# Sliding-window attention and a leaky-ReLU MLP on one core: queries and keys transposed from two row groups of the PE array

## The chip, the cores and the metric

The kernel runs on one NeuronCore of a Trainium2 chip. The core has a matrix engine (PE, whose weight loads are listed apart as PEld), a vector engine (DVE), a scalar engine (ACT), a general engine (POOL) and a queue that issues DMAs (SP); POOL can issue DMAs as well. Each engine works through its own list of instructions in order and waits on semaphores for the others. The metric is device time in microseconds. Before the change it was 356.27 us, the median of 3 runs (355.5 to 356.88).

## The reference

Eight batches of eight heads, 576 tokens, head dimension 64. Each token attends to the tokens at most 32 away; the result goes through a two-layer MLP with a leaky ReLU.

```python
scores = scale * np.matmul(q, k.transpose(0, 1, 3, 2))        # [8, 8, 576, 576], scale = 1/8
mask = np.abs(pos[:, None] - pos[None, :]) <= 32
attn = softmax(np.where(mask, scores, -1e9))
x = np.matmul(attn, v)                                        # to [4608, 512]: heads side by side
h = x @ w_in                                                  # [4608, 2048]
out = np.maximum(0.01 * h, h) @ w_out                         # [4608, 512], float32
```

## The kernel before, in words

Heads are taken in pairs: pair `p` holds heads `p` and `p + 4`, so that the two heads' 64 dimensions fill 128 rows. There are four pairs (`NPAIR`) in each of eight batches (`B`).

**Loads.** `load_qk` (L63 to L74) fetches q and k of a pair into two tiles, `qf` and `kf`, of 96 partitions; partition `i` holds six (`RUN`) consecutive tokens of both heads, two runs of 1536 bytes. Each tile is one DMA of 288 KB on SP's queue. `load_v` (L76 to L86) uses two DMAs, each into 64 partitions. When `behind` is given, a DMA of one element from a weight tile is first put into the tile that will be loaded (L69), so that the load, which overwrites that element, can't start before those weights have landed. Batch 1's q and k are held back in this way behind a part of `w_in`.

**Casts.** `cast_qk` (L163) turns a pair's q and k into bf16 tiles `qb` and `kb`, on POOL; for batches 0 and 1 the q half runs on DVE. The heads' dimensions are brought side by side in the same instruction. `cast_v` (L169) writes v into block-diagonal tiles `vbd`.

**Transposes.** `transposes` (L177 to L208) is a generator that issues its work piece by piece. For each pair and for q, then k, it issues six PE transposes of 96 rows by 128 columns into one PSUM tile `tp`, and ACT copies the tile out: q into `qT` (L195), k into `kT` (L201), from which DVE fills the block-diagonal `kbd` (L204). Each `next` of the generator does q or k of one pair. For batches 0 and 1 `tp` comes from the ring `mmps` of three PSUM buffers that the MLP's matmuls use; for later batches it comes from `tps`, a pool of one buffer of its own.

**Attention.** A step `i` covers half a sequence of one pair. `score(i)` issues five matmuls, ACT's exponential (L226) and POOL's mask product (L230). `weighted(i)` issues two matmuls for the sums (L238, L239), five for the values (L246), DVE's reciprocal (L252) and DVE's product into `xT` (L254).

**MLP.** `h_tile` (L259 to L268) is four matmuls with 256 or 384 token columns and ACT's leaky ReLU; `o_tile` (L270 to L281) is sixteen matmuls of 512 columns, a DVE copy, and the store.

**Order.** Everything is issued in an order written out in the program; there is no scheduler. The first part, from L344 on, is straight-line code for batch 0 and batch 1. After it the MLP is cut into chunks, and before each chunk `step()` (L306) is called as often as a rate and the chunk's needed tokens ask. A step issues the next score, then its own weighted sum, and around them the transposes of the next batch up to the count in `PLAN`, then the casts and loads that `PLAN` lists for later batches. `state["tp"]` counts pieces of the generator, eight per batch.

Of the kernel before, what the change touches and what calls it, by code (L numbers as in the profile page):

```python
# [9 lines left out]
FP32 = mybir.dt.float32  # L10
BF16 = mybir.dt.bfloat16
AF = mybir.ActivationFunctionType
# [4 lines left out]
def kernel(  # L17
# [12 lines left out]
    nc = tc.nc  # L30

    B, H, S, D = q.shape
# [5 lines left out]
    NPAIR = H // 2  # L38
# [20 lines left out]

    qf, kf, vf = {}, {}, {}  # L60
    RUN = S // 96

    def load_qk(b, p, behind=None):  # L63


        for into, src, name in ((qf, q, "qf"), (kf, k, "kf")):
            t = fload.tile([96, 2, RUN * D], FP32, name=f"{name}{p}")
            if behind is not None:
                nc.sync.dma_start(out=t[0:1, 0, 0:1], in_=behind.bitcast(FP32))  # L69
                behind = None  # L70
            nc.sync.dma_start(  # L71
                out=t, in_=src[b, p:H:NPAIR].rearrange("a (p c) d -> p a (c d)", c=RUN),
            )
            into[b, p] = t  # L74

    def load_v(b, p, behind=None):  # L76

# [22 lines left out]
    ident = const.tile([128, 128], BF16)  # L100
# [5 lines left out]
    nc.vector.memset(ones_bd[64:128, 64:128], 1.0)  # L106


    qb = const.tile([96, NPAIR, RUN, 2, D], BF16)
    kb = const.tile([96, NPAIR, RUN, 2, D], BF16)  # L110
# [26 lines left out]
    for lo in (0, 64):  # L137
        w = win[lo:lo + 64]
        nc.gpsimd.affine_select(
            out=w, in_=w, compare_op=ALU.is_ge, fill=0.0,  # L140
# [3 lines left out]
            out=w, in_=w, compare_op=ALU.is_ge, fill=0.0,  # L144
# [15 lines left out]

    qT = {}

    def cast_qk(b, p, q_eng=None):  # L163
        for eng, src, dst in ((q_eng or nc.gpsimd, qf, qb), (nc.gpsimd, kf, kb)):
            eng.tensor_copy(  # L165
                out=dst[:, p], in_=src[b, p].rearrange("p a (c d) -> p c a d", d=D),
            )
# [9 lines left out]
    def transposes(b, first=False):  # L177

        qT[b] = attn.tile([128, NPAIR, S], BF16, name="qT")
        for p in range(NPAIR):  # L180
            for which, src in (("q", qb), ("k", kb)):
                if first:
                    tp = mmps.tile([128, RUN, 96], BF16, name="tp0", tag="mm")
                else:
                    tp = tps.tile([128, RUN, 96], BF16, name="tp")
                for c in range(RUN):
                    nc.tensor.transpose(  # L187
                        tp[:, c],
                        src[:, p, c].rearrange("p a d -> p (a d)"),
                        ident[0:96, 0:96],  # L190
                    )

                tok = tp.rearrange("p c i -> p i c")
                if which == "q":
                    nc.scalar.activation(  # L195
                        out=qT[b][:, p].rearrange("p (i c) -> p i c", c=RUN), in_=tok, func=AF.Copy,
                    )
                else:
                    kT = attn.tile([128, S], BF16, name="kT")
                    kT_v = kT.rearrange("p (i c) -> p i c", c=RUN)  # L200
                    nc.scalar.activation(out=kT_v, in_=tok, func=AF.Copy)  # L201
                    for a in range(2):
                        r = slice(64 * a, 64 * a + 64)
                        nc.vector.tensor_copy(  # L204
                            out=kbd[b % 2][r, p, :, r],
                            in_=kT[r].rearrange("p (n j) -> p n j", j=64),
                        )
                yield  # L208

    probs = {}  # L210

# [3 lines left out]
    def score(i):  # L215
        b, hf, p = where(i)
        ps = scps.tile([128, 1024], FP32, name="ps")
        c0 = 512 - HALF
        for blk, q0, n in WIN[hf]:
            nc.tensor.matmul(  # L220
                ps[:, c0:c0 + n], kbd[b % 2][:, p, blk],
                qT[b][:, p, q0:q0 + n], start=True, stop=True,
            )
# [58 lines left out]


    NC = 2 * NPAIR * B
    state = {"tp": 8, "done": 0}
    t_parts = {}

    PLAN = (
        ((0, 0, 0, 0, 0, 2, 4, 6), ((), (), (), (), (0,), (1, 2), (3,), ()),
         ((), (), (), (), (), (), (0,), (1, 2, 3))),
        ((0, 1, 2, 3, 4, 5, 6, 7), ((0,), (1,), (2,), (3,), (), (), (), ()),
         ((), (), (), (), (0,), (1,), (2,), (3,))),
    )

    def step_transposes(upto):
        while state["tp"] < min(upto, 8 * B):
            b = state["tp"] // 8  # L300
# [43 lines left out]
    first = transposes(0, first=True)  # L344

    def first_pair():
        next(first)
        next(first)

    cast_qk(0, 0, nc.vector)  # L350
    make_masks()
    cast_qk(0, 1, nc.vector)
    first_pair()
    first_pair()
    clear(vbd[0], 2)
    cast_v(0, 0)
    cast_qk(0, 2, nc.vector)
    score(0)
    load_w_in(0, 512)
    first_pair()  # L360
    clear(vbd[0], 3)
    cast_qk(0, 3, nc.vector)
    load_w_in(512, 1024)
    for i in range(NPAIR):
        score(i + 1)
        if i + 1 < NPAIR:
            cast_v(0, i + 1, on_act=True)
        if i < 2:
            load_w_in(1024 + 512 * i, 1536 + 512 * i)
        else:  # L370
            load_w_out(i - 2)
        weighted(i)
        if i == 0:
            first_pair()
    state["done"] = NPAIR


# [10 lines left out]
        if f % 4 == 3:  # L388
            nc.gpsimd.memset(kbd[1][:, f // 4], 0.0)
    for p in range(NPAIR):  # L390
        cast_qk(1, p, nc.vector)
    for p in range(NPAIR):
        load_v(1, p, w_out_bf[0:1, 4, 0:2] if p == 0 else None)
    second = transposes(1, first=True)
    for f in range(FFC):
        h_tile(256, 256, f)
        if f % 4 == 3:
            next(second)
            next(second)
            nc.gpsimd.memset(vbd[1][:, f // 4], 0.0)  # L400
    state["tp"] = 16
    score(8)
    for p in range(NPAIR):
        if p < 3:
# [69 lines left out]
```

The softmax here doesn't subtract the row's maximum and nothing guards it: scores larger than these inputs give would overflow.

## Time and profile before

| what | value |
|---|---|
| median of 3 runs | 356.27 us |
| the profiled execution, and its span | 355.59 us, 353.9 us |
| PE busy, share of the span | 324.3 us, 92% |
| weight loads (PEld) | 208.2 us, 59% |
| DVE, ACT, POOL busy | 211.8, 183.4, 178.7 us |
| DMA packets, MB | 60707, 42.37 MB |
| transposes, q and k (L187) | 2 x 192, 14.4 us busy each, mean 214 ns |
| evictions of q and k on ACT (L195, L201) | 2 x 32, mean 649 and 650 ns |
| POOL casts of k and q (L165) | 32 of 834 ns, 24 of 820 ns |
| median from issue to landing of q, k, v loads | 3.5, 3.9, 3.4 us |

Busy time of PE is a sum of records that overlap, because matmuls are pipelined: one transpose's record lasts 214 ns, while a row of six takes less than half of six times that. How long a row of matmuls really takes is read from the start of one to the start of what follows. The granted clock of PE was full throughout the execution (every digit of the page's clock row is 9).

### The profile page before, as it was taken

To read this page: it belongs to the slowest core of one execution; us is meant where nothing else is said; L and a number is where in the kernel's file an instruction comes from. 1 tells how busy PE (TensorE), PEld (TensorE's weight loads), DVE (VectorE), ACT (ScalarE), POOL (GpSimd) and SP (SyncE) were. 2 spreads that over 40 slices of the span, in tenths; PEclk is the share of its full clock that TensorE was granted. 3 is DMA by queue.
4 is the path that set the end of the run, shared out by engine and by line. 5 is a ranking of instruction groups with operands and counts; after the bars stand their busy time and mean duration, and the time that the engine had idled before them with its cause. 6 is when DMAs were issued, how large, how long until landed. Compare 5 with 4: busy or idle time off the path is not lost.

```text
span 353.9 us, 6635 instructions
## 1 busy us (share of the span) xinstructions
PE 324.3 (92%) x2600; PEld 208.2 (59%) x2624; DVE 211.8 (60%) x242; ACT 183.4 (52%) x363; POOL 178.7 (51%) x213
## 2 busy tenths in 40 slices
PE   2658998999989898999999898999999999999995
PEld 1437864584957655656656555656656656555472
DVE  5588647757686877645653778554676676630101
ACT  5765862292845637518527527716528517326060
POOL 7797676578765766524543568533655423200000
PEclk9999999999999999999999999999999999999999
DMA  8999986599995274342453265340010010020101
GB/s 187 214 205 236 269 162 182 144 201 235 209 255 146 58 222 133 69 126 88 140 162 70 63 177 165 88 124 33 0 61 30 2 61 31 5 86 0 61 31 59
DMA packets 60707, 42.37 MB, mean 120 GB/s; under 512 B 39684, under 2 KB 56068, under 8 KB 60676
## 3 DMA queue, kind: packets, MB, share of 16 engines
q1 hardware_dynamic: 56388, 37.76, 42.7%
q0 software_dynamic: 4288, 4.20, 7.2%
q8 instruction: 20, 0.33, 0.4%
q14 instruction: 11, 0.09, 0.1%
HBM read 36.70 MB, written 9.44 MB: 130 GB/s over the span
## 4 chain that ended last, share of the span: by engine, by line
PE 77%; DMA 7%; DVE 6%; POOL 4%; SPq 2%; issue 2%; ACT 1%; DVEq 0%; POOLq 0%; ACTq 0%
PE mm L273 33%; PE mm L264 31%; DMA kf<-in_k_dram 7%; DVE r L252 5%; PE x L246 3%; PE tp L187 3%; PE ps L220 3%; PE s L238 2%; PE s L239 2%; SPq L71 1%; POOL vbd L175 1%; POOL vbd L400 1%; SPq L82 1%; DVE xT L254 1%; POOL pr L230 1%
## 5 line engine op out<-in xcount | busy, mean ns | idle before, releaser
L252 DVE RECIPROCAL r<-s 128x288 f32<-128x288 f32 x64 | 125.1, 1954 | 38.5 <-PE s L239 38.2
L230 POOL TENSOR_TENSOR pr<-e,mask 128x544 bf16<-128x544 bf16 x64 | 77.7, 1213 | 115.0 <-ACT e L226 114.7
L264 PE MATMUL mm<-xT,w_in_bf 128*128 128x384 bf16 (+1 forms) x896 | 132.7, 304 | 0.9 <-ACT kT L201 0.8
L268 ACT ACTIVATE gT<-mm 128x384 bf16<-128x384 f32 (+1 forms) x224 | 99.0, 445 | 63.0 <-PE mm L264 58.6
L273 PE MATMUL mm<-w_out_bf,gT 128*128 128x512 bf16 x552 | 126.8, 379 | 1.3
L264 PEld LDWEIGHTS <-w_in_bf 128*128 128x128 bf16 x896 | 86.6, 98 | 38.0 <-issue 1.3
L273 PEld LDWEIGHTS <-gT 128*128 128x128 bf16 x576 | 54.9, 98 | 61.1
L226 ACT ACTIVATE e<-ps 128x544 bf16<-128x544 f32 x64 | 39.8, 622 | 77.6 <-PE ps L220 77.6
L280 DVE COPY o_sb<-mm 128x512 f32<-128x512 f32 x36 | 24.9, 691 | 66.8 <-PE mm L273 66.8
L204 DVE COPY kbd<-kT 64x576 bf16<-64x576 bf16 x64 | 28.4, 444 | 18.2 <-ACT kT L201 17.6
L175 POOL CAST vbd<-vf 64x576 bf16<-64x576 f32 x58 | 38.3, 661 | 1.9
L254 DVE TENSOR_TENSOR xT<-x,r 128x288 bf16<-128x288 f32 x64 | 29.3, 458 | 7.0 <-PE mm L264 0.5
L165 POOL CAST kb<-kf 96x768 bf16<-96x768 f32 x32 | 26.6, 834 | 9.5 <-DMA kf<-in_k_dram 9.5
L246 PE MATMUL x<-pr,vbd 128*128 128x128 bf16 (+2 forms) x320 | 26.9, 217 | 2.0 <-POOL vbd L175 1.0
L220 PE MATMUL ps<-qT,kbd 128*128 128x128 bf16 (+2 forms) x320 | 27.3, 219 | 0.3
L238 PE MATMUL s<-pr,ones_bd 128*128 128x288 bf16 x64 | 19.0, 297 | 8.7 <-DVE r L252 7.0
L220 PEld LDWEIGHTS <-kbd 128*128 128x128 bf16 x320 | 21.1, 102 | 8.1 <-issue 0.6
L195 ACT ACTIVATE qT<-tp 128x576 bf16<-128x576 bf16 x32 | 20.8, 649 | 9.6 <-PE tp L187 9.0
L246 PEld LDWEIGHTS <-vbd 128*128 128x128 bf16 x320 | 21.4, 101 | 7.1 <-issue 2.8
L201 ACT ACTIVATE kT<-tp 128x576 bf16<-128x576 bf16 x32 | 20.8, 650 | 8.9 <-PE tp L187 7.9
L187 PE MATMUL tp<-ident,qb 96*128 96x96 bf16 x192 | 14.4, 214 | 8.5 <-DVE qb L165 6.7
L165 POOL CAST qb<-qf 96x768 bf16<-96x768 f32 x24 | 19.7, 820 | 0.0
(31 smaller groups left out, 107.7 us busy)
## 6 DMA issues: line engine op xcount, KB each, us to landing
qf<-in_q_dram SPq DMA_DIRECT2D x32, 288.0 KB, 3.5
kf<-in_k_dram SPq DMA_DIRECT2D x32, 288.0 KB, 3.9
vf<-in_v_dram SPq DMA_DIRECT2D x64, 144.0 KB, 3.4
out_dram<-o_sb SPq DMA_DIRECT2D x36, 256.0 KB, 2.2
w_in_bf<-in_moe_w_in_dram POOLq DMA_DIRECT2D x8, 256.0 KB, 6.4
w_out_bf<-in_moe_w_out_dram POOLq DMA_DIRECT2D x4, 512.0 KB, 13.5
qf<-w_in_bf SPq DMA_DIRECT2D x1, 0.0 KB
vf<-w_out_bf SPq DMA_DIRECT2D x1, 0.0 KB
```

Source lines behind the costliest of these rows:

```text
L165: eng.tensor_copy(out=dst[:, p], in_=src[b, p].rearrange("p a (c d) -> p c a d", d=D),)
L175: nc.gpsimd.tensor_copy(out=vbd[b % 2][r, p, :, r], in_=vf[b, p][r])
L204: nc.vector.tensor_copy(out=kbd[b % 2][r, p, :, r], in_=kT[r].rearrange("p (n j) -> p n j", j=64),)
L220: nc.tensor.matmul(ps[:, c0:c0 + n], kbd[b % 2][:, p, blk], qT[b][:, p, q0:q0 + n], start=True, stop=True,)
L226: nc.scalar.activation(out=e, in_=ps[:, 512 - HALF:512 - HALF + NCOL], func=AF.Exp, scale=scale,)
L230: nc.gpsimd.tensor_mul(pr, e, mask[hf])
L246: nc.tensor.matmul(x[:, a:a + n], vbd[b % 2][:, p, blk, :], pr[:, c0:c0 + n], start=(n_ == 0), stop=(n_ == len(WIN[hf]) - 1), skip_group_c ...
L252: nc.vector.reciprocal(r, s)
L254: nc.vector.tensor_mul(xT[:, p, t0:t0 + HALF], x, r)
L264: nc.tensor.matmul(h[:, 0:n], w_in_bf[:, c, ts(f, 128)], xT[:, c, ds(t0, n)], start=(c == 0), stop=(c == DMC - 1),)
L268: nc.scalar.activation(out=gT[t0][:, f, 0:n], in_=h[:, 0:n], func=AF.Prelu, alpha=0.01)
L273: nc.tensor.matmul(o, gT[t0][:, f, ts(j, 128)], w_out_bf[:, f, :], start=(f == 0), stop=(f == FFC - 1),)
```

## The change

q and k of a pair now share one tile, `qkf`: q on partitions 0 to 63, k on 64 to 127. A partition holds nine consecutive tokens of both heads, two runs of 2304 bytes, and `RUN` is 9. The bf16 copies share `qkb` likewise. One cast on POOL covers both; for batches 0 and 1 it is split into 64 rows on DVE and 64 on POOL. With `behind`, both halves get the one-element DMA.

A transpose now takes 64 rows and gives 64 columns. q's transposes are placed in rows 0 to 63 of the PE array and k's in rows 64 to 127, and are issued in turn, nine of each, into two PSUM tiles. These come from the ring `mmps` in all batches; the ring has four buffers, and the pool `tps` is gone. Each `next` of the generator does a whole pair, so the counts in `PLAN` and `state["tp"]` are halved, and `step` issues transposes in one place, after the weighted sum.

```diff
-    mmps = ctx.enter_context(tc.tile_pool(name="mmps", bufs=3, space=PS))
+    mmps = ctx.enter_context(tc.tile_pool(name="mmps", bufs=4, space=PS))
...
-    tps = ctx.enter_context(tc.tile_pool(name="tps", bufs=1, space=PS))
-    RUN = S // 96
+    RUN = S // 64
...
-        for into, src, name in ((qf, q, "qf"), (kf, k, "kf")):
-            t = fload.tile([96, 2, RUN * D], FP32, name=f"{name}{p}")
+        t = fload.tile([128, 2, RUN * D], FP32, name=f"qkf{p}")
+        for w, src in enumerate((q, k)):
             if behind is not None:
-                nc.sync.dma_start(out=t[0:1, 0, 0:1], in_=behind.bitcast(FP32))
-                behind = None
+                nc.sync.dma_start(out=t[64 * w:64 * w + 1, 0, 0:1], in_=behind.bitcast(FP32))
             nc.sync.dma_start(
-                out=t, in_=src[b, p:H:NPAIR].rearrange("a (p c) d -> p a (c d)", c=RUN),
+                out=t[64 * w:64 * w + 64],
+                in_=src[b, p:H:NPAIR].rearrange("a (p c) d -> p a (c d)", c=RUN),
             )
...
-    def cast_qk(b, p, q_eng=None):
-        for eng, src, dst in ((q_eng or nc.gpsimd, qf, qb), (nc.gpsimd, kf, kb)):
-            eng.tensor_copy(
-                out=dst[:, p], in_=src[b, p].rearrange("p a (c d) -> p c a d", d=D),
+    def cast_qk(b, p, split=False, eng=None):
+        parts = ((nc.vector, 0, 64), (nc.gpsimd, 64, 128)) if split else ((eng or nc.gpsimd, 0, 128),)
+        for e, lo, hi in parts:
+            e.tensor_copy(
+                out=qkb[lo:hi, p],
+                in_=qkf[b, p][lo:hi].rearrange("p a (c d) -> p c a d", d=D),
             )
...
         for p in range(NPAIR):
-            for which, src in (("q", qb), ("k", kb)):
-                if first:
-                    tp = mmps.tile([128, RUN, 96], BF16, name="tp0", tag="mm")
-                else:
-                    tp = tps.tile([128, RUN, 96], BF16, name="tp")
-                for c in range(RUN):
+            tp = [mmps.tile([128, RUN, 64], BF16, name=f"tp{w}", tag="mm") for w in range(2)]
+            for c in range(RUN):
+                for w in range(2):
+                    r = slice(64 * w, 64 * w + 64)
                     nc.tensor.transpose(
-                        tp[:, c],
-                        src[:, p, c].rearrange("p a d -> p (a d)"),
-                        ident[0:96, 0:96],
+                        tp[w][:, c],
+                        qkb[r, p, c].rearrange("p a d -> p (a d)"),
+                        ident[r, r], tile_position=(64 * w, 0),
                     )
...
-        ((0, 0, 0, 0, 0, 2, 4, 6), ((), (), (), (), (0,), (1, 2), (3,), ()),
+        ((0, 0, 0, 0, 0, 1, 2, 3), ((), (), (), (), (0,), (1, 2), (3,), ()),
...
-        ((0, 1, 2, 3, 4, 5, 6, 7), ((0,), (1,), (2,), (3,), (), (), (), ()),
+        ((0, 0, 1, 1, 2, 2, 3, 3), ((0,), (1,), (2,), (3,), (), (), (), ()),
...
-        if b > 0:
-            upto = 8 * (b + 1) + PLAN[b > 1][0][r]
-            step_transposes(max(upto - 1, 8 * (b + 1)))
         if i + 1 < NC and i != 7:
             score(i + 1)
         weighted(i)
         if b > 0:
-            step_transposes(upto)
+            step_transposes(NPAIR * (b + 1) + PLAN[b > 1][0][r])
...
-    cast_qk(0, 0, nc.vector)
+    cast_qk(0, 0, split=True)
```

The evictions on ACT, the copies into `kbd` on DVE, and everything after them are as before, each once per pair for q and once for k.

More of the change, by code (lines that the diff above doesn't have):

```diff
@@ L53 @@
     PS = bass.MemoryType.PSUM
[L54 removed]
+    mmps = ctx.enter_context(tc.tile_pool(name="mmps", bufs=4, space=PS))
     scps = ctx.enter_context(tc.tile_pool(name="scps", bufs=1, space=PS))
     xps = ctx.enter_context(tc.tile_pool(name="xps", bufs=1, space=PS))
[L57 to L61 removed]
+    qkf, vf = {}, {}
+    RUN = S // 64
     def load_qk(b, p, behind=None):
[L66 to L67 removed]
+        t = fload.tile([128, 2, RUN * D], FP32, name=f"qkf{p}")
+        for w, src in enumerate((q, k)):
             if behind is not None:
[L69 to L70 removed]
+                nc.sync.dma_start(out=t[64 * w:64 * w + 1, 0, 0:1], in_=behind.bitcast(FP32))
             nc.sync.dma_start(
[L72 removed]
+                out=t[64 * w:64 * w + 64],
+                in_=src[b, p:H:NPAIR].rearrange("a (p c) d -> p a (c d)", c=RUN),
             )
[L74 removed]
+        qkf[b, p] = t
     def load_v(b, p, behind=None):
@@ L106 @@
     nc.vector.memset(ones_bd[64:128, 64:128], 1.0)
-    qb = const.tile([96, NPAIR, RUN, 2, D], BF16)
-    kb = const.tile([96, NPAIR, RUN, 2, D], BF16)
+    qkb = const.tile([128, NPAIR, RUN, 2, D], BF16)
     kbd = [const.tile([128, NPAIR, NB, 128], BF16, name=f"kbd{i}") for i in range(2)]
@@ L175, in cast_v, with transposes @@
                 nc.gpsimd.tensor_copy(out=vbd[b % 2][r, p, :, r], in_=vf[b, p][r])
-    def transposes(b, first=False):
+    def transposes(b):
         qT[b] = attn.tile([128, NPAIR, S], BF16, name="qT")
         for p in range(NPAIR):
-            for which, src in (("q", qb), ("k", kb)):
-                if first:
-                    tp = mmps.tile([128, RUN, 96], BF16, name="tp0", tag="mm")
-                else:
-                    tp = tps.tile([128, RUN, 96], BF16, name="tp")
-                for c in range(RUN):
+            tp = [mmps.tile([128, RUN, 64], BF16, name=f"tp{w}", tag="mm") for w in range(2)]
+            for c in range(RUN):
+                for w in range(2):
+                    r = slice(64 * w, 64 * w + 64)
@@ L187, in transposes @@
                     nc.tensor.transpose(
-                        tp[:, c],
-                        src[:, p, c].rearrange("p a d -> p (a d)"),
-                        ident[0:96, 0:96],
-                    )
[L193 to L207, printed above, removed]
@@ L208, in transposes @@
-                yield
+                        tp[w][:, c],
+                        qkb[r, p, c].rearrange("p a d -> p (a d)"),
+                        ident[r, r], tile_position=(64 * w, 0),
+                    )
+            nc.scalar.activation(
+                out=qT[b][:, p].rearrange("p (i c) -> p i c", c=RUN),
+                in_=tp[0].rearrange("p c i -> p i c"), func=AF.Copy,
+            )
+            kT = attn.tile([128, S], BF16, name="kT")
+            nc.scalar.activation(
+                out=kT.rearrange("p (i c) -> p i c", c=RUN),
+                in_=tp[1].rearrange("p c i -> p i c"), func=AF.Copy,
+            )
@@ L210 @@
+            for a in range(2):
+                r = slice(64 * a, 64 * a + 64)
+                nc.vector.tensor_copy(
+                    out=kbd[b % 2][r, p, :, r],
+                    in_=kT[r].rearrange("p (n j) -> p n j", j=64),
+                )
+            yield
     probs = {}
@@ L284 @@
     NC = 2 * NPAIR * B
-    state = {"tp": 8, "done": 0}
+    state = {"tp": NPAIR, "done": 0}
     t_parts = {}
     PLAN = (
-        ((0, 0, 0, 0, 0, 2, 4, 6), ((), (), (), (), (0,), (1, 2), (3,), ()),
+        ((0, 0, 0, 0, 0, 1, 2, 3), ((), (), (), (), (0,), (1, 2), (3,), ()),
          ((), (), (), (), (), (), (0,), (1, 2, 3))),
-        ((0, 1, 2, 3, 4, 5, 6, 7), ((0,), (1,), (2,), (3,), (), (), (), ()),
+        ((0, 0, 1, 1, 2, 2, 3, 3), ((0,), (1,), (2,), (3,), (), (), (), ()),
          ((), (), (), (), (0,), (1,), (2,), (3,))),
@@ L298, in step_transposes @@
     def step_transposes(upto):
-        while state["tp"] < min(upto, 8 * B):
-            b = state["tp"] // 8
+        while state["tp"] < min(upto, NPAIR * B):
+            b = state["tp"] // NPAIR
             if b not in t_parts:
@@ L342, in load_w_out @@
         nc.gpsimd.dma_start(out=w_out_bf[:, c, :], in_=w_out_r[:, c, :])
[L344 to L348, printed above, removed]
-    cast_qk(0, 0, nc.vector)
+    first = transposes(0)
+    cast_qk(0, 0, split=True)
     make_masks()
-    cast_qk(0, 1, nc.vector)
-    first_pair()
-    first_pair()
+    cast_qk(0, 1, split=True)
+    next(first)
+    next(first)
     clear(vbd[0], 2)
     cast_v(0, 0)
-    cast_qk(0, 2, nc.vector)
+    cast_qk(0, 2, split=True)
     score(0)
     load_w_in(0, 512)
-    first_pair()
+    next(first)
     clear(vbd[0], 3)
-    cast_qk(0, 3, nc.vector)
+    cast_qk(0, 3, split=True)
     load_w_in(512, 1024)
@@ L373 @@
         if i == 0:
-            first_pair()
+            next(first)
     state["done"] = NPAIR
@@ L390 @@
     for p in range(NPAIR):
-        cast_qk(1, p, nc.vector)
+        cast_qk(1, p, split=True)
     for p in range(NPAIR):
         load_v(1, p, w_out_bf[0:1, 4, 0:2] if p == 0 else None)
-    second = transposes(1, first=True)
+    second = transposes(1)
     for f in range(FFC):
@@ L398 @@
             next(second)
-            next(second)
             nc.gpsimd.memset(vbd[1][:, f // 4], 0.0)
-    state["tp"] = 16
+    state["tp"] = 2 * NPAIR
     score(8)
```

## The prediction

> **What bounds the kernel now.** I read the share of each engine by stretch first, since the page's averages mix a start that waits for loads with a long stretch that doesn't. In these windows the columns are busy us and instructions of PE, weight loads, DVE, ACT and POOL, then granted clock, DMA share, GB/s.
>
> ```profile
> 0.00:28.00 28.00, 13.17 (x111) 9.32 (x112) 18.14 (x27) 18.07 (x25) 22.87 (x37) 1.00 1.14 202
> 28.00:54.00 26.00, 24.74 (x239) 19.30 (x238) 16.78 (x22) 18.01 (x44) 18.04 (x20) 1.00 1.04 219
> 54.00:70.00 16.00, 14.76 (x108) 8.45 (x111) 12.29 (x13) 3.07 (x6) 9.23 (x12) 1.00 0.57 161
> 70.00:354.00 284.00, 271.65 (x2147) 171.10 (x2166) 164.58 (x184) 144.22 (x290) 128.60 (x147) 1.00 0.39 100
> ```
>
> Up to 28 us PE is busy less than half the time while the DMA engines are full (share above 1); from 70 us on PE is busy 271.65 of 284 us. So there are two prices: a delay of the loads early, and PE time later. Next the chain that ended last, in order of time (start us, us, what), for the early part:
>
> ```profile
> 8.27 7.67 DMA kf<-in_k_dram
> ...
> 15.99 0.82 POOL kb L165
> ...
> 30.73 15.97 DMA kf<-in_k_dram
> ...
> 46.76 0.82 POOL kb L165
> 47.58 3.64 POOL vbd L400 x4
> ```
>
> The last k load of batch 0 (8.27 to 15.9) and that of batch 1 (30.73 to 46.7) set the pace, each followed by POOL's k cast, and POOL's queue behind it (clears, mask products, v casts) reaches PE. Last, the timeline of PE where it is full, and where two steps come back to back:
>
> ```profile
> 200.21 0.42 PE L187 MATMUL tp<-ident,qb 96*128 96x96 bf16 x6
> 201.37 0.41 PE L187 MATMUL tp<-ident,kb 96*128 96x96 bf16 x6 [0.74 <-ACT qT L195]
> 201.62 0.41 PE L220 MATMUL ps<-qT,kbd 128*128 128x96 bf16 x5
> 202.31 0.30 PE L238 MATMUL s<-pr,ones_bd 128*128 128x288 bf16 x1 [0.29 <-DVE r L252]
> ...
> 206.56 0.40 PE L220 MATMUL ps<-qT,kbd 128*128 128x96 bf16 x5
> 206.80 0.29 PE L238 MATMUL s<-pr,ones_bd 128*128 128x288 bf16 x1
> ...
> 207.27 0.42 PE L187 MATMUL tp<-ident,qb 96*128 96x96 bf16 x6
> 207.53 3.62 PE L273 MATMUL mm<-w_out_bf,gT 128*128 128x512 bf16 x16
> ```
>
> Six transposes take 0.26 us, start to next start (207.27 to 207.53), 576 columns; five score matmuls, 544 columns, 0.24 us. Both are 0.44 to 0.45 ns a column, though the five include a 64-column matmul: weight loads hide, even behind the narrow ones, and entering or leaving the 96-row transposes costs nothing.
>
> [...] the stretch that loads v, into 64 rows, moves less than the first q and k loads into 96 rows, though v's runs are also shorter (256 against 1536 bytes).
>
> ```profile
> 2.00:6.00 4.00, 0.66 (x6) 0.45 (x6) 2.56 (x5) 2.45 (x4) 2.56 (x5) 1.00 1.01 265
> 48.00:53.00 5.00, 4.87 (x40) 3.06 (x41) 1.99 (x5) 2.95 (x8) 5.00 (x6) 1.00 1.14 194
> ```
>
> **Part by part.** *Batch 0's loads.* Each q and k load keeps its 288 KB (0.295 MB), now into 64 rows. Four of them at 265 GB/s are 4.45 us; at v's 194, 6.1 us (+1.6). The two later pairs, 0.59 MB each at 233 GB/s (the window 8 to 11 us) 2.53 us, become 3.04 (+0.5 each): +2.6 for the last k load. [...] I take +1.9.
>
> *POOL's k cast* goes from 96x768 to 64x1152. POOL casts of 576 and 768 elements take 661 and 834 ns, 0.9 ns an element, so 1152 take 1.18 us: +0.35, paid on the chain after the last k load of batch 0 and of batch 1: +0.7. The DVE half rises likewise from about 0.56 (its shorter casts in the timeline) to 0.75 us; DVE isn't the late one there. From batch 2 on one POOL cast of 1.18 us replaces two of 0.83: 0.48 us saved, 24 times, hidden, as POOL is busy 128.6 of 284 us. Were POOL the bound, it would be worth 11 us.
>
> *The second one-element copy.* Loads of batch 1 are held behind a copy out of w_in. Now:
>
> ```profile
> 22.77 0.73 SPq L69 DMA_DIRECT2D qf<-w_in_bf  x1
> 27.39 0.33 SPq L71 DMA_DIRECT2D qf<-in_q_dram  x1
> ```
>
> SP issues it until 23.5 and stands until it has landed, 27.39: 3.9 us. The changed program puts a second one before k's first load, which overwrites the same row and so waits for it. Behind it on SP stand seven loads of batch 1 and all of v: they go out about 0.3 + 0.7 + 3.9 = 5 us later. The engines have weights to move meanwhile, so most of that is work done in another order; but when the weights are through, the rest of q and k runs alone at some 200 GB/s instead of in the 271 of the stretch 31 to 45. I take +1.2 for the last k of batch 1; 0 if nothing idles, +5 if nothing covers it.
>
> *Transposes on PE.* 384 of 96 columns become 576 of 64: 12 x 96 = 18 x 64 = 1152 columns a head pair, 0.52 us before and after if the row groups run in turn; 0.26 if two always overlap. Around each group of 18 stand two changes of tiling mode. Price unknown: 0 at best; 0.10 us each if only the first weight load comes into view (its row: 98 ns median)[...]. I take 0.10. Of the 28 pairs after batch 0 some five fall into back-to-back steps where PE waits for DVE's reciprocal anyway, so 23 x 2 x 0.10 = +4.6.
>
> *The PSUM ring.* The private buffer goes, so the k transposes no longer wait for the q eviction: 2.2 us in three places in the waits. In two of them (119 and 201 us) the reciprocal's wait follows at once and grows instead; I count -0.9, at most -2.2. In return each pair takes two of four ring buffers, held until ACT has evicted both (0.65 us each, behind an exp of 0.62). With h tiles of 384 columns (four matmuls of 162 ns, 0.65 us) PE meets them already freed; with 256 (0.44 us) it may stand 0.1 to 0.3 us: +0.3 in all, at most 3. A fourth buffer itself is worth nothing, as PE hardly waits for the ring now (0.9 us at L264).
>
> *Order.* A pair's transposes now come together after the step's weighted sum, where k's came before the next score. Casts run at least a step ahead, loads likewise, so PE waits for neither: nothing.
>
> Sum: 1.9 + 0.7 + 1.2 + 4.6 - 0.9 + 0.3 = +7.8 us, on the profiled execution's 355.59 (span 353.9 and 1.7 around it): 363.4. The median shown is 0.7 above that execution: 364.1, say 364.
>
> **Rivals.** *Row groups overlap* and the switch doesn't show: 0.26 instead of 0.52 us, 23 x -0.26 = -6.0, with +3.2 from the other terms: 356.3 - 2.8 = 353.5; if early loads are also no slower, about 351. It decides once a pair's transposes, switches included, are under 0.38 us. [...] *Switch free, no overlap*: only the early terms, 356.3 + 3.2 = 359.5. *Cancelling*: half the overlap pays for the switches, the loads cost half: 357.
>
> **How the numbers follow.** Likeliest (early delay and a visible switch, 361 to 369): 0.52. Switch free 0.15, overlap 0.13[...], cancelling 0.08. About 0.5%, 1.8 us, is what a measurement of this kernel can tell from no change. Faster: most of the overlap case, 0.12. Same: the cancelling case and edges, 0.10. Slower: the rest, 0.78. Range 355.5 to 371.5[...].
>
> **What would show it.** The last k load of batch 0 lands near 18 us instead of 15.9; POOL's k casts are near 1.18 us; SP stands about 4 us twice; the last k cast of batch 1 begins near 50 to 51 us instead of 46.8. From the first transpose of a pair to the next matmul PE takes 0.7 us: 0.5 or less means overlap or a free switch[...]. I am wrong if q and k load at the old rate into 64 rows, or if two transposes start a few ns apart.

## The result and the profile after

The changed kernel takes 361.33 us, the median of 4 runs (359.59 to 362.54), against 356.13 us (355.5 to 356.88) before on the same chip. The ratio is 1.0141, 95% interval 1.0094 to 1.0189: slower by 5.2 us. Its profiled execution took 360.98 us, with a span of 359.3 us, which is 5.4 us over the one of before.

The share of each engine by stretch, in the kernel after. The columns are busy us and instructions of PE, weight loads, DVE, ACT and POOL, then granted clock, DMA share and GB/s; the last line is the stretch of the first q and k loads.

```profile
0.00:28.00 28.00, 10.51 (x130) 7.42 (x130) 19.51 (x25) 17.11 (x24) 22.48 (x36) 1.00 1.10 190
28.00:54.00 26.00, 20.83 (x236) 16.52 (x236) 18.74 (x20) 16.07 (x41) 16.05 (x16) 1.00 1.04 204
...
70.00:354.00 284.00, 274.33 (x2319) 169.27 (x2340) 166.87 (x186) 142.44 (x291) 119.43 (x124) 0.99 0.42 102
2.00:6.00 4.00, 0.00 (x0) 0.00 (x0) 3.35 (x5) 2.30 (x3) 1.89 (x4) 1.00 0.93 213
```

PE lost 2.7 us of work in the first stretch and 3.9 in the second; the DMA engines were nearly as busy as before (shares of 1.10 for 1.14 and 0.93 for 1.01) and moved less (190 for 202 GB/s, 213 for 265 in the stretch 2 to 6 us). From 70 us on the granted clock is 0.99, where it was 1.00 before.

The chain that ended last, in order of time (start us, us, what), in the kernel after:

```profile
17.19 1.34 DVE qkb L164
...
40.50 10.49 DMA qkf<-in_k_dram
...
51.04 1.16 POOL qkb L164
...
58.97 0.41 PE x L245 x5
```

The same values' matmul in the chain of before:

```profile
54.14 0.41 PE x L246 x5
```

The last k load of batch 1 is issued at 40.50 instead of 30.73 us; the cast behind it starts at 51.04 instead of 46.76, and the first values' matmul after it at 58.97 instead of 54.14: 4.8 us are lost by then. Earlier, DVE's cast of q stands on the chain, which it did not before. That part of the chain is inferred: it reaches the last k load through POOL's clears of `kbd`, while SP's own timeline shows the loads following one another from 36.43 us on. Whether the cast costs anything is left to an experiment.

To see where the rest came, take the same weight loads of the MLP in both traces and subtract their start times. Each row is one kernel minus the kernel before; the last four are experiments that come below.

| kernel | at 58.5 us of before | at 98 | at 147 | at 339 | from 58.5 to 339 |
|---|---|---|---|---|---|
| after | +4.84 | +3.22 | +5.39 | +5.48 | +0.64 |
| one one-element copy instead of two | +3.56 | +1.93 | +2.39 | +2.51 | -1.05 |
| counts moved up one step | +4.95 | +3.31 | +2.82 | +1.86 | -3.09 |
| before, with ring and grouped order | +0.08 | -1.43 | +0.94 | +1.42 | +1.34 |
| the same, counts moved up one step | 0.00 | -1.52 | -2.04 | -2.58 | -2.58 |

So after loses nearly all of it by 58.5 us, then wins 1.6 us, loses 2.2 again between 98 and 147, and keeps that. The kernel with one copy differs from it in batch 1's loads alone, and it loses only 0.5 us between 98 and 147. What happens in that second loss is in the timeline of PE after, around two steps that come back to back:

```profile
138.62 0.40 PE L219 MATMUL ps<-qT,kbd 128*128 128x64 bf16 x5 [0.38 <-ACT e L225]
140.06 0.30 PE L237 MATMUL s<-pr,ones_bd 128*128 128x288 bf16 x1 [1.03 <-DVE r L251]
...
140.94 0.44 PE L186 MATMUL tp<-ident,qkb 64*128 64x64 bf16 x18
141.31 4.45 PE L263 MATMUL mm<-xT,w_in_bf 128*128 128x384 bf16 x16
```

PE waits for the exponential, then for the reciprocal, and the sixteen matmuls that follow take longer than twenty did elsewhere (3.42 us). The windows of the same stretch of after say why; the third number from the end is the granted clock, as a share of full speed:

```profile
138.00:140.00 2.00, 0.64 (x11) 0.34 (x7) 1.96 (x1) 1.20 (x3) 1.35 (x2) 1.00 0.75 200
...
142.00:144.00 2.00, 2.00 (x8) 0.88 (x6) 1.72 (x4) 1.10 (x3) 1.39 (x3) 0.50 0.76 200
```

From 141.4 to 144.9 us, 3.413 us in the trace, PE ran at half its clock, which costs 1.7 us. The kernel before and the kernel with one copy have no such stretch in their traces. (The kernels before and after both start at half clock, although pages and windows show full clock there: h tile matmuls of 256 columns start 213 ns apart until 30.1 us before and 32.2 us after, and 109 ns apart from then on.)

And the pair of transposes itself, in the timeline of PE after:

```profile
133.74 0.44 PE L186 MATMUL tp<-ident,qkb 64*128 64x64 bf16 x18
134.11 3.42 PE L263 MATMUL mm<-xT,w_in_bf 128*128 128x384 bf16 x20
```

From the first transpose to the next MLP matmul is 0.37 us. The single records give more: a k transpose starts 3 to 5 ns after its q transpose, and the next couple 24 to 26 ns later (35 after the first couple), so from the first start to the last are 0.245 us. From the matmul before to the first transpose are 152 ns where whole-array neighbours have 56, and from the last transpose to the next matmul 123 where they have 29: going to the row groups and back cost 0.095 us each.

### The profile page after: what moved, and what is told of

The parts are those of the page before. It is cut to its first block, busy times and chain, and to the rows that moved or that the text cites. A ratio compares the mean times of both kernels' runs of the same rounds, so it can differ in the third digit from the quotient of the medians.

```text
span 359.3 us, 6996 instructions
## 1 busy us (share of the span) xinstructions
PE 321.6 (90%) x2792; PEld 201.5 (56%) x2816; DVE 216.4 (60%) x242; ACT 180.1 (50%) x363; POOL 170.5 (47%) x189
## 4 chain that ended last, share of the span: by engine, by line
PE 79%; DVE 8%; POOL 5%; DMA 4%; issue 2%; ACT 1%; SPq 0%; DVEq 0%; POOLq 0%; ACTq 0%
PE mm L263 33%; PE mm L272 33%; DVE r L251 5%; DMA qkf<-in_k_dram 4%; PE x L245 4%; PE ps L219 3%; PE tp L186 3%; PE s L237 2%; PE s L238 2%; POOL vbd L390 1%; POOL vbd L175 1%; POOL pr L229 1%; POOL qkb L164 1%; POOL kbd L380 1%; DVE xT L253 1%
## 5 line engine op out<-in xcount | busy, mean ns | idle before, releaser
L267 ACT ACTIVATE gT<-mm 128x384 bf16<-128x384 f32 (+1 forms) x224 | 97.2, 448 | 65.1 <-PE mm L263 61.3
L164 POOL CAST qkb<-qkf 128x1152 bf16<-128x1152 f32 (+1 forms) x32 | 36.6, 1145 | 11.5 <-DMA qkf<-in_k_dram 11.4
L186 PE MATMUL tp<-ident,qkb 64*128 64x64 bf16 x576 | 15.9, 197 | 16.9 <-DVE qkb L164 12.3
L186 PEld LDWEIGHTS <-qkb 64*128 64x128 bf16 x576 | 11.4, 98 | 21.6 <-DVE qkb L164 13.3
```

The costliest lines, as they stand in the source:

```text
L164: e.tensor_copy(out=qkb[lo:hi, p], in_=qkf[b, p][lo:hi].rearrange("p a (c d) -> p c a d", d=D),)
L186: nc.tensor.transpose(tp[w][:, c], qkb[r, p, c].rearrange("p a d -> p (a d)"), ident[r, r], tile_position=(64 * w, 0),)
L267: nc.scalar.activation(out=gT[t0][:, f, 0:n], in_=h[:, 0:n], func=AF.Prelu, alpha=0.01)
```

## The experiments

All ran beside the kernel before, whose medians were 356.1 to 356.2 us.

**One one-element copy instead of two.** The loads of batch 1 are held once, as before.

```diff
                 nc.sync.dma_start(out=t[64 * w:64 * w + 1, 0, 0:1], in_=behind.bitcast(FP32))
+                behind = None
```

> The second one-element copy is left out; k's first load of batch 1 stands behind q's on SP's queue. Theory (SP's second stand of about 5 us leaves q and k to run alone once the weights are through): SP stands once, all eight loads go out within 4 us as before the change, POOL's last k cast of batch 1 begins near 47.5 us instead of 51.0, and the time falls by 2 to 3 us, to about 358.5. Rival (the DMA engines only do the same work in another order): the last cast still begins near 51 and the time stays within 0.5 us of 361.

Measured: 360.59 us (358.07 to 361.43), ratio 1.0129 (1.0102 to 1.0156). In the chain of this kernel the last k load of batch 1 reads:

```profile
34.98 14.74 DMA qkf<-in_k_dram
```

All eight loads are out by 34.98 instead of 40.50 us, yet the last cast starts at 49.77 instead of 51.04. The second copy costs 1.3 us there, although it delays the issue by 5.5; it seems that the rest is transfer time that has to be spent anyway. That lies between the theory and the rival. In the times, executions of like granted clock differ by 0.8 to 1.5 us (at full clock 358.07 here and 359.59 after, at 0.995 360.2 and 360.98).

**Two copies in the kernel before**, the mirror of it, with 96-row loads.

```diff
-                behind = None
+                if name == "kf":
+                    behind = None
```

> The kernel before with a second one-element copy, ahead of k's first load of batch 1, and nothing else. Theory (a second stand of SP delays seven loads, and q and k then run alone when the weights are through): POOL's last k cast of batch 1 begins 1 to 2.5 us later than 46.8, and the time grows by 1 to 2.5 us. Rival (with loads into 96 rows the tail is fast enough to be absorbed): within 0.5 us of before.

Measured: 356.95 us (355.94 to 358.63, 20 runs), ratio 1.0025 (1.0012 to 1.0038): +0.85 us. SP's timeline shows it stand twice, for 3.7 and 4.9 us after the issue has ended:

```profile
22.52 0.72 SPq L69 DMA_DIRECT2D qf<-w_in_bf  x1
...
27.42 0.61 SPq L69 DMA_DIRECT2D kf<-w_in_bf  x1
32.89 0.32 SPq L72 DMA_DIRECT2D kf<-in_k_dram  x1
```

The last k cast begins at 47.59 for 46.76, and that 0.83 us stays to the end. This lies between the two values that were expected.

**Loads alone, by rows.** Attention and MLP are left out; only transfers of q in several shapes, each of 0.295 MB, and one element read from each by DVE when it lands.

```diff
...
+    phase(96, 2, run6, False)
+    phase(64, 2, run9, False)
+    phase(64, 2, run9, True)
+    phase(64, 2, run9, True, True)
+    phase(64, 3, run6, True)
+    phase(128, 1, run9, False)
...
```

The numbers are rows and runs a row; `run9` are runs of 2304 bytes, `run6` of 1536. The first `True` sends every second load to rows 64 to 127, the second puts it on ACT's queue.

> Loads alone: six phases of eight loads of 288 KB (the fifth of 288 KB as well) from q, each phase begun when the one before has landed; attention and MLP are left out, and what is stored is not the result. Phases: 96 rows with two runs of 1536 bytes; rows 0-63 with two runs of 2304; the same in rows 0-63 and 64-127 in turn; the same with the second half issued by ACT; 64 rows in turn with three runs of 1536; 128 rows with one run of 2304. Theory (rows set the rate): 96 and 128 rows move 270 GB/s or more, all four of 64 rows about 200 to 230. Rival (the length of the runs sets it): both phases of 1536 bytes are alike and fast, and the 128 rows with 2304 are as slow as the 64.

DVE's timeline in this kernel gives a landing per line: two for one half, two for the halves in turn with short runs, two for 128 rows.

```profile
24.71 0.15 DVE L53 COPY seen<-big 64x1 f32<-64x1 f32 x1 [1.32 <-DMA big<-in_q_dram]
26.19 0.15 DVE L53 COPY seen<-big 64x1 f32<-64x1 f32 x1 [1.33 <-DMA big<-in_q_dram]
...
51.82 0.15 DVE L53 COPY seen<-big 64x1 f32<-64x1 f32 x1 [1.05 <-DMA big<-in_q_dram]
53.15 0.15 DVE L53 COPY seen<-big 64x1 f32<-64x1 f32 x1 [1.18 <-DMA big<-in_q_dram]
...
64.40 0.15 DVE L53 COPY seen<-big 128x1 f32<-128x1 f32 x1 [0.60 <-DMA big<-in_q_dram]
65.11 0.15 DVE L53 COPY seen<-big 128x1 f32<-128x1 f32 x1 [0.56 <-DMA big<-in_q_dram]
```

One half lands a load every 1.49 us over six loads, 198 GB/s; the halves in turn every 1.23 to 1.26 us, 235 to 239 GB/s, with long runs and with short ones alike; 128 rows every 0.74 us, 400 GB/s. Landings of the halves in turn alternate between about 1.18 and 1.33 us. In these phases the rows set the rate, not the runs. The part with 96 rows can't be read, because its loads had to wait for the clears of their tiles, and the part with the second half on ACT's queue was held up by the order of its issues.

**k of batch 0 on ACT's queue**, so that the two halves go out side by side.

```diff
-            nc.sync.dma_start(
+            (nc.scalar if b == 0 and w == 1 else nc.sync).dma_start(
```

> k's four loads of batch 0 are issued by ACT, so that q's and k's packets are in the engines side by side. Theory [...]: the first 4 us of loading move 280 GB/s or more instead of about 230, POOL's k casts of batch 0 begin about 1 us earlier; the time falls by 0.5 to 1 us. Rival (the rate has another limit, such as the reads): the rate stays near 230 and the casts don't move.

Measured: 359.96 us (358.99 to 362.29), ratio 1.0113 (1.0071 to 1.0155). The window of the first loads moves what it moved from one queue:

```profile
2.00:6.00 4.00, 0.00 (x0) 0.00 (x0) 2.16 (x4) 2.48 (x3) 3.01 (x5) 1.00 0.93 213
```

k's casts come earlier (4.82 and 7.56 us instead of 6.16 and 8.91) and q's later (6.11 and 8.78 instead of 4.81 and 7.44). Issuing from one queue is not what makes the loads slow. The 1.4 us in the medians lie within the scatter of the two kernels.

**Cast read in another order.** DVE's casts stand at 1.34 us after, where 0.75 was forecast. Here the heads are the outermost dimension, two instead of nine.

```diff
-                out=qkb[lo:hi, p],
-                in_=qkf[b, p][lo:hi].rearrange("p a (c d) -> p c a d", d=D),
+                out=qkb[lo:hi, p].rearrange("p c a d -> p a c d"),
+                in_=qkf[b, p][lo:hi].rearrange("p a (c d) -> p a c d", d=D),
```

> The cast walks head, run, dimension instead of run, head, dimension; the same values land in the same places. Theory (the 1.34 us DVE cast is slow because its outermost count became 9[...]): DVE casts of 64x1152 fall to about 0.7 us, the second reciprocal begins near 20.6 us instead of 21.8, and the time falls by 1 us. Rival (DVE is slow [...]because of the 64 rows): DVE casts stay at 1.3 us and nothing moves.

Measured: 361.69 us (358.95 to 362.59), ratio 1.0139 (1.0093 to 1.0185), so no different from after. The timeline of DVE in this kernel:

```profile
4.70 0.75 DVE L164 CAST qkb<-qkf 64x1152 bf16<-64x1152 f32 x1
...
17.48 1.35 DVE L164 CAST qkb<-qkf 64x1152 bf16<-64x1152 f32 x1
```

The order does set the speed: the cast at 4.70 us, which ends before POOL's first cast begins (6.03), takes 0.75 us, where after took 1.34 for the same cast (4.81 us, POOL's from 6.16). But the two late casts of batch 0 gain little or nothing (1.24 us at 13.31, 1.35 at 17.48); at these places POOL casts the k half in the kernel after (13.06 and 17.39 us, 1.15 us each). Theory and rival were each half right, and the time didn't move.

**All of q, then all of k**: the row groups are kept, most of the overlap is taken away.

```diff
-            for c in range(RUN):
-                for w in range(2):
+            for w in range(2):
+                for c in range(RUN):
```

> The same 18 transposes in the same two row groups, but nine of q and then nine of k, so that no two overlap. Theory (overlap halves the streaming, 0.26 us for 0.52, and two changes of tiling mode give back 0.19 of it): a pair takes about 0.72 us instead of 0.465, and the time grows by 4 to 6 us. Rival (the 4 ns between q's and k's starts are only how the records are drawn): a pair still takes about 0.47 and the time is within 1 us of 361.

Measured: 364.95 us (364.12 to 367.64), ratio 1.0257 (1.021 to 1.0303). Timeline of PE:

```profile
136.16 0.60 PE L186 MATMUL tp<-ident,qkb 64*128 64x64 bf16 x18
136.69 3.42 PE L263 MATMUL mm<-xT,w_in_bf 128*128 128x384 bf16 x20
```

From first transpose to next matmul 0.53 us for 0.37: the alternation is worth 0.16 us a pair, 3.8 us over 24 pairs, and the medians differ by 3.6, a little under the 4 to 6 expected. Of all the kernels this one comes nearest to what the forecast took the change to be; even so its pair takes 0.53 us where the forecast had 0.7.

**Counts moved up one step.** In the batches from 2 on, transposes are due one step earlier.

```diff
-        ((0, 0, 1, 1, 2, 2, 3, 3), ((0,), (1,), (2,), (3,), (), (), (), ()),
+        ((0, 1, 1, 2, 2, 3, 3, 4), ((0,), (1,), (2,), (3,), (), (), (), ()),
```

> The changed kernel with its transposes one step earlier (counts 0, 1, 1, 2, 2, 3, 3, 4). Theory (PE drops to half clock for 3.4 us after a stretch of about as long with little PE work, and that stretch is the back-to-back steps of which the first has no transposes): the transposes fill the stretch, the granted clock is 0.999 or more in every run, and the median falls by about 2 us, to 359. Rival (the half clock comes with the change of tiling mode itself): the clocks stay between 0.99 and 0.995 in most runs and the median near 361.

Measured: 357.24 us (356.69 to 357.64, 8 runs), ratio 1.003 (1.0016 to 1.0043): 4.1 us under after, with the same early loss (+4.95 at 58.5 us). Two lines of the waits of PE in after (`s` are the sums, which wait for the reciprocal; `ps` the scores, which wait for the exponential):

```profile
PE s L237 <- DVE r L251: 9.1, 8, 1.3
...
PE ps L219 <- ACT e L225: 1.7, 5, 0.4
```

The numbers are us in total, times, and the longest. In the kernel before, the first of the two reads

```profile
PE s L238 <- DVE r L252: 7.0, 8, 1.2
```

In the kernel with the counts moved up the waits for the reciprocal are much the same as after (8.9 us), and the five waits for an exponential, 1.66 us, are gone: the transposes now stand between two scores that come back to back, where PE has nothing else to do. In the timeline of PE of this kernel,

```profile
137.79 0.44 PE L186 MATMUL tp<-ident,qkb 64*128 64x64 bf16 x18
138.24 0.40 PE L219 MATMUL ps<-qT,kbd 128*128 128x64 bf16 x5
```

and before the change only q's half stood there, and PE still waited 0.29 us between the two:

```profile
134.57 0.42 PE L187 MATMUL tp<-ident,qb 96*128 96x96 bf16 x6
135.11 0.40 PE L220 MATMUL ps<-qT,kbd 128*128 128x64 bf16 x5
```

The clock too is full in the profiled execution, where after lost 1.7 us. Two of the eight executions still had a mean clock of 0.995 and 0.993, against the theory, but were no slower than the rest (357.33 and 357.31 us).

**The order without the row groups.** The kernel before, with the ring of four and the grouped order of the change, but 96-row transposes of the whole array and all loads and casts as before.

```diff
-    mmps = ctx.enter_context(tc.tile_pool(name="mmps", bufs=3, space=PS))
+    mmps = ctx.enter_context(tc.tile_pool(name="mmps", bufs=4, space=PS))
...
-        ((0, 1, 2, 3, 4, 5, 6, 7), ((0,), (1,), (2,), (3,), (), (), (), ()),
+        ((0, 0, 2, 2, 4, 4, 6, 6), ((0,), (1,), (2,), (3,), (), (), (), ()),
...
-            step_transposes(max(upto - 1, 8 * (b + 1)))
...
```

> The kernel before with only the ring and the order of the change: mmps of four buffers serves the transposes of all batches, q and k of a pair are transposed together, after the weighted sum, in every second step, as whole-array transposes of 96 rows. Theory (order makes the stretches with little PE work): clocks of 0.991 to 0.995 in most runs, time 356.5 to 358. Rival (the tiling mode makes the half clock): clock 1.0 in all runs and a time of about 355, as q's wait is gone.

Measured: 357.41 us (355.29 to 359.81, 20 runs), ratio 1.003 (1.0009 to 1.0051). Windows of its profiled execution:

```profile
102.00:104.00 2.00, 0.73 (x9) 0.53 (x10) 1.90 (x3) 0.60 (x1) 2.00 (x3) 1.00 1.10 233
104.00:106.00 2.00, 2.00 (x17) 1.24 (x15) 1.90 (x2) 1.19 (x2) 2.00 (x3) 0.50 1.07 309
```

There is the half clock again, in a kernel without any row groups, and the five waits for the exponential, 1.7 us, as well. Its 20 executions are sorted by their mean granted clock: 8 at 1.0 have a median of 355.6 us, 7 at 0.995 (one half-clock stretch) 357.5, and 5 at 0.99 (two) 359.0. A stretch costs 1.5 to 1.9 us. The executions of after fit: 359.59 at 1.0, 360.98 at 0.995, 361.67 and 362.54 at 0.991. The kernel before stood at 0.998 or above throughout.

**The same with the counts moved up one step.**

```diff
-        ((0, 0, 2, 2, 4, 4, 6, 6), ((0,), (1,), (2,), (3,), (), (), (), ()),
+        ((0, 2, 2, 4, 4, 6, 6, 8), ((0,), (1,), (2,), (3,), (), (), (), ()),
```

> The kernel before with its 96-row transposes of the whole array, the ring of four and the grouped order, with the counts 2, 2, 4, 4, 6, 6, 8 a step earlier; against the kernel with row groups from batch 2 on and the same counts (353.28 us; from its first h tile to the end it gained 3.0 us on the kernel before). Theory, that the order is worth the rest and the row groups little more than 1 us (24 pairs, 0.505 us falling to 0.465): no exponential wait ahead of a score, hardly a half-clock stretch, a gain of about 2.0 us from the first h tile to the end, and some 354 us as this kernel's early part is that of before. Rival, that the row groups earn the gain: less than 1 us gained, 355.5 us or more. Second rival, that row groups earn nothing at all: a gain of 3.0 us and 353 us.

Measured: 353.35 us (352.99 to 354.99), ratio 0.9934 (0.9914 to 0.9954): faster than before by 2.8 us, with nothing of the row groups (but with the ring of four, which was not tried apart from the order). No wait for ACT is left in the list of PE's waits. The 2.58 us gained from 58.5 us on lie between the theory (2.0) and its second rival (3.0): the order, with the ring, earns nearly all of it, and the row groups less than was reckoned.

**Row groups from batch 2 on.** Batches 0 and 1 load, cast and transpose 96 rows as before, later ones as in the change; first with its counts, then with the counts moved up.

```diff
-        for into, src, name in ((qf, q, "qf"), (kf, k, "kf")):
-            t = fload.tile([96, 2, RUN * D], FP32, name=f"{name}{p}")
+        u = fload.tile([128, 4 * RUN0 * D], FP32, name=f"qkf{p}")
+        if b < 2:
+            for n, (into, src) in enumerate(((qf, q), (kf, k))):
+                t = u[0:96, 2 * RUN0 * D * n:2 * RUN0 * D * (n + 1)].rearrange("p (a f) -> p a f", a=2)
...
+        t = u[:, 0:2 * RUN * D].rearrange("p (a f) -> p a f", a=2)
+        for w, src in enumerate((q, k)):
...
```

> Batches 0 and 1 are loaded, cast and transposed as before the change (96 rows, one gate), batches 2 to 7 as in the change; the ring of four and the order of the change stay. Theory (the delay lies in batches 0 and 1, 4.8 us by the trace, and later the change gains about 1 us that the half clock takes back): the first MLP matmuls stand where they stood before, and the time is 355 without a half-clock stretch, near 357 with one. Rival (the delay of the early part would have been absorbed, and the loss lies in batches 2 to 7): still 359 or more at full clock.

Measured: 356.82 us (355.2 to 359.1, 13 runs), ratio 1.0028 (1.0009 to 1.0048). Its profiled execution has the five waits for the exponential, 1.7 us, and two half-clock stretches again, so these belong to the counts and not to the early part. The two executions at full clock took 355.2 and 356.82 us, so the rival's 359 is ruled out.

```diff
-        ((0, 0, 1, 1, 2, 2, 3, 3), ((0,), (1,), (2,), (3,), (), (), (), ()),
+        ((0, 1, 1, 2, 2, 3, 3, 4), ((0,), (1,), (2,), (3,), (), (), (), ()),
```

> As the one before, with the transposes one step earlier. Theory: no early delay, no half clock; 355, about 1 us faster than before the change. Rival (half clock comes with the tiling mode): clocks under 0.996, 357.

Measured: 353.28 us (352.73 to 353.84), ratio 0.9925 (0.9905 to 0.9946). Both versions are about 1 us late at 58.5 us (+1.07 for the second). The delay is there already when batch 0's last k load has landed: POOL's cast of it begins at 17.01 us in the second and 17.54 in the first, where before it began at 15.99. These loads have 96 rows as before but lie in shared tiles; why they land later stays open. From 58.5 us to the end the second gains 3.10 us, where the whole-array kernel with the same counts gains 2.58. The changed kernel with the counts moved up gains 3.09, and so does the next kernel below (3.10), so the row groups earn 0.5 us by the traces. The medians, 353.28 and 353.35, don't tell the two kernels apart, as the late start takes it back. From the start of the matmul before a pair to the start of the matmul after it are 0.520 us here and 0.568 there; 24 pairs would give 1.1, but where PE would wait anyway it earns nothing.

**One copy and the counts moved up**, both in the changed kernel.

```diff
                 nc.sync.dma_start(out=t[64 * w:64 * w + 1, 0, 0:1], in_=behind.bitcast(FP32))
+                behind = None
...
-        ((0, 0, 1, 1, 2, 2, 3, 3), ((0,), (1,), (2,), (3,), (), (), (), ()),
+        ((0, 1, 1, 2, 2, 3, 3, 4), ((0,), (1,), (2,), (3,), (), (), (), ()),
```

> The changed kernel with one gate and with the transposes one step earlier. Theory (the two effects add: 1.3 to 1.5 us from the gate, and no half clock): clocks of 0.998 or more and a time near 355.8, still with the slower first loads and casts. Rival (the gate's gain was covered by something else): 357.2, as with the earlier transposes alone.

Measured: 356.35 us (355.0 to 357.03, 20 runs), ratio 1.0004 (0.9993 to 1.0015). That is 0.9 us under the kernel with the counts alone, so the two effects add, if with less from the copy than the 1.3 to 1.5 expected. With two lines mended the change is worth nothing, up or down: what its loads lose early the order gives back.

## Why the prediction was right and where it was wrong

The direction was right, and 361.33 lies in the range, 2.7 us under the forecast; the upper end of the range, 371.5, was an estimate for a dearer switch, which wasn't shown. That the sum came so near is luck: the transposes came out 5.7 us below their term, and the early part, the ring and the order together some 3.4 above theirs.

- *Batch 0's loads, casts, second copy: right.* Forecast +3.8 in all, of which +1.9 for the loads was an estimate under the +2.6 that v's rate gives; measured +4.8 at 58.5 us. The loads moved 213 GB/s for 265, the ratio 0.80; the loads alone show that rows set it: 198 GB/s for one half, 19 to 21% more for the halves in turn, 400 GB/s for 128 rows. POOL's casts took 1.145 us (1.18 forecast). k's last cast of batch 0 began at 17.39 for 15.99, +1.4 where +1.9 was forecast for the load; that of batch 1 at 51.04, in the forecast's 50 to 51. The second copy is worth 0.8 to 1.5 (1.2 forecast). Which of these makes the 1 us over the forecast was not separated.
- *DVE's cast at 0.75, "DVE isn't the late one there": wrong.* It took 1.34 us and came onto the chain. Its casts have nine as outermost dimension, and a price read off casts with six didn't hold for nine. With another order of reading 0.75 came back for the first cast, but not for the two late casts of batch 0 (1.24 and 1.35), and the time stayed: what the cast cost was not shown.
- *Transposes, +4.6: wrong.* The failed step is the choice of 0.52 us of streaming after the change. The sign that was named for it appeared: starts 3 to 5 ns apart. Eighteen take 0.245 us, and with two switches at 0.095 each (0.10 forecast, right) a pair is 0.05 us cheaper than before, some -1.1 us over 23 pairs. From one couple to the next it is 24 to 26 ns. The rival "row groups overlap" had the mechanism without the switches.
- *The ring, -0.9: not seen apart.* The waits for the q eviction went (2.2 us), those for the reciprocal grew by as much (7.0 to 9.1).
- *Order, "nothing": wrong.* It asked only whether casts and loads were in time. It didn't ask what the transposes had been filling. With the counts of the change, in which transposes come due in every second step, five back-to-back scores wait for the exponential (1.66 us), and PE's idle time lies so close together that half-clock stretches follow (none to two in an execution of after, 1.5 to 1.9 us each). In the kernels with the counts moved up those waits are gone and half-clock stretches are rare (mean clock under 0.997 in 6 of their 38 executions, in 12 of 20 of the whole-array kernel without the move). That whole-array kernel has both without the row groups.

By the lists of waits the terms are +4.8 early, -1.1 transposes, +1.7 exponential, +1.75 half clock and -0.1 ring and reciprocal, +7.1 in all, against +5.4 in the profiled executions. The lists miss part of what PE waited for before the change. I estimate its idle time from the starts of the matmuls, at 0.42 ns a column (512 columns take 216 ns): between 60 and 339 us it is 12.1 us before and 12.2 in the kernel with one copy, which has the later part of after without a half-clock stretch. Where that kernel waits 2.5 us for exponentials (counted in the same way), the kernel before had waited 2.7 us for q's eviction, and 1.4 in short gaps beside transposes (0.19 to 0.29 us each, at 73, 78, 83, 102, 134 and 216 us). So +4.8 early, +0.1 idle, -1.1 transposes and +1.7 half clock make +5.5: the order of the change cost hardly any idle time on balance, and what it cost was the clock.

What goes ahead of the half clock can be read from the traces together. In the trace of after the changes of the clock lie 109.226, 3.413 and 215.04 us apart, that is 32, 1 and 63 times 3.413 us; in that of before 324.266 us, 95 times. With windows of 3.413 us laid from these changes on, I estimate from the starts of the matmuls (0.42 ns a column) the share of each window in which PE streamed, in all thirteen traces of whole kernels. In after it is 0.33 in the window from 138.03 to 141.44 us, which the half clock follows; the next lowest is 0.41 (from 206.3 us), with full clock behind it. The seven half-clock stretches inside these kernels follow windows with a share of 0.32 to 0.36; of some 1200 windows no other one ahead of a kernel's end is below 0.38. In after and in the kernel with one copy there are five gaps where the share would fall to 0.30 to 0.33 if a window lay right on them: in the trace of after one did, in that of the other none, as its windows lay astride (0.43 or more). With the order before the change, and with the counts moved up, no stretch of 3.413 us from 60 us on is below 0.41, wherever it is laid. Why a few executions of the latter still had a mean clock of 0.993 to 0.995 isn't shown, as none of those was traced.

## What to carry to other kernels

When a piece of work is moved, ask what stood idle where it was: here transposes that filled a wait between two dependent steps (0.45 us of them with the counts moved up, where PE had waited 0.38 between the two scores) cost next to nothing, and the same transposes one step later cost their own time, the wait (1.7 us over five) and, in some executions, the clock (1.5 to 1.9 us a stretch). Look not only at how long an engine idles but at how close together the pauses lie: here as much idle time as before cost 1.7 us more once it was bunched. Row groups that alternate overlapped here (18 transposes in 0.245 us), but each visit paid for going in and out (0.19 us), so they want long visits; and a tile cut into halves of 64 rows paid for it in the transfers (235 to 239 GB/s for the halves in turn, 400 for 128 rows) where these were the bound. Try the order alone before the clever layout: here the order, with the ring of four, was worth 2.8 us, and the row groups 0.5.

## What the hardware showed that was not expected

- Two transposes of different row groups start 3 to 5 ns apart, a couple each 29 ns; going from whole-array matmuls to these row groups costs 0.095 us, and so does going back (152 ns for 56, and 123 for 29, in the trace of after).
- With all of q ahead of all of k, a pair took only 0.16 us more (0.53 for 0.37), where eighteen of 28 ns one after another (a 64-column matmul of after starts 28 to 29 ns ahead of the next) would take 0.26 more than the 0.245 measured. By this estimate some of the eighteen still overlap.
- Half a clock for exactly 3.413 us (in after, from 141.44 us), within a kernel in which PE is busy 90% of the time, after a window of the same length in which PE streamed for 0.33 of the time by my estimate (0.32 to 0.36 over seven such stretches); after windows with 0.38 and more the clock stayed full. The same gaps in the trace of the kernel with one copy, with the windows astride, had no such stretch.
- A DVE cast of 64x1152 from float32 to bf16 takes 1.34 us with nine as outermost dimension (after), 0.75 with two (at 4.70 us, in the kernel with the cast read in another order), and 1.24 and 1.35 there for the two late ones of batch 0.
